# Attention + max3-MoE on one Trainium2 core: the rounding of a finished pv moved one step later, and left keys times v moved to column halves of TensorE

## Chip, cores and metric

One Trainium2 chip, 1 core. The metric is device microseconds of one execution. The kernel before takes 641.23 us (median of 3 runs, 640.48 to 642.72).

## The reference

Attention with a relative-position bias over 4 batches, 8 heads, 576 positions, head size 64, in fp32, and then an MoE-like layer on the 2304 tokens:

```
scores = q @ k.T / 8 + bias            # bias: a small MLP of log-distances, one 576x576 map per head
attn   = exp(scores - max); attn /= sum + 1e-9
x      = attn @ v                      # tokens x 512
h      = max(x @ w1, x @ w2, x @ w3)   # 2304 x 768
out    = h @ w_out                     # 2304 x 512
```

## The kernel before

The program runs in three stages: bias maps (to about 57 us), attention (to about 340 us), and the MoE layer. The change touches attention alone.

Attention works on 16 **units**, one for each pair of heads and batch. A unit has five **steps**, t0 to t4, one for each tile of 128 queries. Steps t0 to t3 handle 128 queries of both heads; t4 handles the last 64 queries of both heads as one tile. So a step has two score tiles (h0 and h1), and t4 has one. The program is written out in a fixed order for each engine (`step`, L325), and engines work through their own lists in that order. A step n does, across engines:

- TensorE: `front` (L234), the score matmuls **s** of step n, in three terms because q and k are split into a rounded part and a remainder; then `flip` (L286, L295), the transposes **tp** and **lp** of the step three back; then, if some are queued, two or three **pairs** of pv matmuls (L311, L314).
- VectorE: `shift` (L244), which reads s out of PSUM, adds the bias and finds the extreme (**sn**, **nm**), once per head; the sum's reciprocal **rc** of the step before (L263, L264); a copy of transposed tiles to **et** (L359). Every third step of the later attention also has two operations that convert MoE weights (L385 to L401).
- ScalarE: the exponentials **e** (L256) and copies to et (L341, L357). GpSimd: the product e times rc (L267) and the splitting of the next unit's q and k (L201, L203).

**pv**, the product with v, is done in two groups per unit: queries 0 to 255 (group 0, 256 wide) and 256 to 575 (group 1, 320 wide). A group is queued after the flip of its last tile and consists of five pairs: four chunks of 128 keys and one of the 64 left keys. A pair is two matmuls, one per head, which write to the lower and the upper 64 partitions of the one PSUM buffer `pv` (there is one, of one bank; all eight banks are in use). Group 1 of a unit runs in steps t3 (three pairs) and t4 (two) of the next unit, group 0 in t0 (three) and t1 (two) of the next. So one group ends in t4 and the next begins in t0; the other ends in t1 and the next begins in t3.

The four chunks use 128 rows of TensorE and 64 columns per head (tiles of 128 x 64, L311). The left keys lie on partitions 0 to 63 for one head and 64 to 127 for the other, so their pair uses 64 rows and 64 columns per head (L314). After a group's fifth pair, at the end of the same step, ScalarE rounds pv to **xhi** (L317) and VectorE writes the remainder **xlo** (L318). v of the next unit is loaded in t4 (`load_v`, L206).

Of the kernel before, what the change touches and what calls it, by code (L numbers as in the profile page):

```python
# [9 lines left out]
F32 = mybir.dt.float32  # L10
# [3 lines left out]
ALU = mybir.AluOpType  # L14
# [5 lines left out]
def kernel(  # L20
# [12 lines left out]
    nc = tc.nc  # L33
    B, H, S, D = v.shape
# [3 lines left out]
    NTQ = S // 128  # L38
    LB = 128 * NTQ
    LEFT = S - LB  # L40
# [6 lines left out]
    psum = ctx.enter_context(tc.tile_pool(name="psum", bufs=1, space=PSUM))  # L47
    dram = ctx.enter_context(tc.tile_pool(name="dram", bufs=1, space=DRAM))

    def ps_s(name):  # L50
        return psum.tile([128, 2, 512], F32, tag="s", bufs=2, name=name)
# [6 lines left out]
    xhi = []  # L58
    xlo = []
# [97 lines left out]
    def load_bias(hp, t):  # L157
        if t < NTQ:
            nc.sync.dma_start(out=bias_t[t], in_=bias_rows(128 * t, 128, 2 * hp, 0, S, 2))
        else:  # L160
            nc.sync.dma_start(out=bias_t[t][0:LEFT], in_=bias_rows(LB, LEFT, 2 * hp, 0, S))
            nc.sync.dma_start(out=bias_t[t][64:64 + LEFT, 0:LB], in_=bias_rows(LB, LEFT, 2 * hp + 1, LEFT, LB))
            nc.sync.dma_start(out=bias_t[t][64:64 + LEFT, LB:S], in_=bias_rows(LB, LEFT, 2 * hp + 1, 0, LEFT))
# [3 lines left out]
    units = [(hp, b) for hp in range(HP) for b in range(B)]  # L167
# [7 lines left out]
    class Attention:  # L175
        def __init__(self, pool):
            self.pool = pool
            self.data = {}
            self.st = {}
            self.et = {}  # L180
            self.pvq = []
            bias_t.extend(pool.tile([128, 2, S], F32, name=f"bias{t}", bufs=1) for t in range(NTQ))
            bias_t.append(pool.tile([128, S], F32, name="biasm", bufs=1))

# [21 lines left out]
        def load_v(self, un):  # L206
            pool, (hp, b) = self.pool, units[un]
            vt = pool.tile([128, NTQ, 2, D], F32, tag="vt", bufs=2, name=f"vt{un}")
            vl = pool.tile([128, D], F32, tag="vl", bufs=2, name=f"vl{un}")
            for h in range(2):  # L210
                main, left = (0, LB) if h == 0 else (LEFT, 0)
                src = v[b, 2 * hp + h]
                nc.sync.dma_start(out=vt[:, :, h], in_=src[main:main + LB].rearrange("(c p) d -> p c d", p=128))
                nc.sync.dma_start(out=vl[64 * h:64 * h + LEFT], in_=src[left:left + LEFT])
            self.data[un].update(vt=vt, vl=vl)

        def heads(self, n):
# [80 lines left out]
                nc.tensor.transpose(lp[0:64], e2[:, LB:S], ident)  # L298
            return tps, (el[:, c0:c0 + m], lp[:, 0:m])

        def queue_pv(self, un, c0, w, ea, el):
            hp, b = units[un]
            u = self.data[un]
            pv = psum.tile([128, w], F32, tag="pv", bufs=1, name=f"pv{un}_{c0}")

            def pair(c):
                def run():
                    for h in range(2):
                        p = slice(64 * h, 64 * h + 64)
                        if c < NTQ:  # L310
                            nc.tensor.matmul(pv[p], lhsT=u["vt"][:, c, h], rhs=ea[:, c, h],  # L311
                                             start=(c == 0), stop=False)
                        else:
                            nc.tensor.matmul(pv[p], lhsT=u["vl"][p], rhs=el[p], start=False, stop=True)  # L314
                    if c == NTQ:
                        r = slice(b * S + c0, b * S + c0 + w)
                        nc.scalar.copy(xhi[hp][:, r], pv)  # L317
                        nc.vector.tensor_tensor(out=xlo[hp][:, r], in0=pv, in1=xhi[hp][:, r].bitcast(F32),  # L318
                                                op=ALU.subtract)
                return run  # L320

            self.wait = True
            self.pvq.extend(pair(c) for c in range(NTQ + 1))

        def step(self, n, more=None):  # L325
            m, f = n - 1, n - LAG
            nh = 0
            if n < NSTEP:
                un, t = sched[n]
                hp, b = units[un]  # L330
                if t == 0 and un + 2 < len(units):
                    self.load_qk(un + 2)
                if t == 4 and un + 1 < len(units):
                    self.load_v(un + 1)
                nh = self.heads(n)
                self.front(n)
                self.shift(n, 0)
            back = 0 <= f < NSTEP
            if back:
                tps, left = self.flip(f)  # L340
                nc.scalar.copy(*tps[0])  # L341
            if nh:
                self.expo(n, 0)
            if nh > 1:
                self.shift(n, 1)
            if n < NSTEP and b == B - 1 and hp + 1 < HP:
                load_bias(hp + 1, t)
            if 0 <= m < NSTEP:
                self.norm(m)
            if nh > 1:  # L350
                self.expo(n, 1)
            if n < NSTEP and un + 1 < len(units):
                if t == 0:
                    self.splits = self.prep(un + 1)
                next(self.splits, None)
            if back:
                nc.scalar.copy(*left)  # L357
                if len(tps) > 1:
                    nc.vector.tensor_copy(*tps[1])  # L359
            if more is not None:  # L360
                for _ in range(2):
                    next(more, None)
            k = 3 if len(self.pvq) >= 3 else 2
            run, self.pvq = self.pvq[:k], self.pvq[k:]
            for x in run:
                x()
            if back:
                un, t = sched[f]
                g = 0 if t < TS else 1
                w = 128 * TS if g == 0 else S - 128 * TS  # L370
                del self.st[f]
                if t in (TS - 1, NS - 1):
                    self.queue_pv(un, 128 * TS * g, w, *self.et)
# [32 lines left out]
    def load_w(pool, wpool, f):  # L406
        for i, m in enumerate((mw1, mw2, mw3)):
            hi = pool.tile([128, KDM * 128], F32R, tag=f"wh{i}", bufs=1, name=f"wh{i}_{f}")
            lo = pool.tile([128, KDM * 128], F32R, tag=f"wl{i}", bufs=1, name=f"wl{i}_{f}")
            wf[i, f] = (hi, lo)  # L410
            src = m[:, 256 * f:256 * f + 256].rearrange("(c p) f -> p c f", p=128)
            yield from convert(wpool, src, hi, lo, f"{i}_{f}")
# [72 lines left out]
    with tc.manual_schedule():  # L485
        nc.vector.memset(signm, 0x80000000)
        warm = const.tile([128, 256], F32, name="warm")
        nc.vector.memset(warm, 0.0)
        wps = ps_s("wps")
        for _ in range(5):  # L490
            nc.tensor.matmul(wps[:, 0, 0:256], lhsT=warm[:, 0:128], rhs=warm, start=True, stop=True)
        apool = tc.alloc_tile_pool(name="attn_p", bufs=1, side="right")
        at = Attention(apool)
        n = 0
        with tc.tile_pool(name="bias_p", bufs=1) as bp:
            for g, _ in enumerate(bias_stage(bp)):
                if g == 0:
                    at.load_qk(0)
                    at.load_v(0)
                    first = at.prep(0)  # L500
                if 5 <= g < 9:
                    next(first)
                if g == 16:
                    at.load_qk(1)
                if g in (10, 18, 26, 34):
                    load_bias(0, g // 8 - 1)
                if g >= NG:
                    at.step(n)
                    n += 1
            load_bias(0, NTQ)  # L510
        xpool = ctx.enter_context(tc.tile_pool(name="xpool", bufs=1, reuse_waits="tile"))
        wpool = ctx.enter_context(tc.tile_pool(name="wpool", bufs=1, reuse_waits="tile"))
        xhi.extend(xpool.tile([128, NT], F32R, name=f"xhi{i}") for i in range(HP))
        xlo.extend(xpool.tile([128, NT], F32R, name=f"xlo{i}") for i in range(HP))
        w0 = load_w(wpool, wpool, 0)
        while n < NSTEP + LAG:
            at.step(n, w0 if n >= NSTEP - 57 and n % 3 == 0 else None)
            n += 1
        while at.pvq:
            at.pvq.pop(0)()  # L520
        for _ in w0:
            pass
        apool.release()
        with tc.tile_pool(name="moe_p", bufs=1, reuse_waits="tile") as mp:
            for _ in moe(mp, wpool):
                pass
# [54 lines left out]
```

## Time and profile before

| | |
|---|---|
| runs | 641.23 us median, 640.48 to 642.72 |
| profiled execution, its own time | 641.89 us |
| its span in the profile | 640.0 us |
| TensorE busy | 612.2 us, 96% of the span |
| VectorE, ScalarE, GpSimd busy | 61%, 43%, 29% |
| mean granted TensorE clock | 0.984 of full speed |

Busy shares are means over three different stages. What an edit of attention is worth is read from the timeline of a step: which wait ends last there. In the views, PE is TensorE's matmuls, PEld its weight loads, DVE is VectorE, ACT ScalarE, POOL GpSimd, SPq the queue that issues DMAs.

### The profile page before, as it was taken

What the parts mean: (1) busy time and instruction counts of PE and PEld (TensorE: products, weight loads), DVE (VectorE), ACT (ScalarE), POOL (GpSimd) and SP (SyncE); (2) the same over time, 40 slices, a digit from 0 to 9 for tenths busy, and PEclk for the clock granted to TensorE, in tenths of its full rate; (3) what the DMA queues carried; (4) which work ended last, traced back from release to release, by engine and by line L of the source; (5) the groups of instructions that cost most, each with busy time, mean ns of one, the idle gap of its engine ahead of it and who ended that gap; (6) DMA issues with size and microseconds to landing.
All of it is one profiled execution on the core that took longest, in us unless ns stands there. A gap on an engine that the chain in (4) does not pass through costs nothing.

```text
span 640.0 us, 11424 instructions
## 1 busy us (share of the span) xinstructions
PE 612.2 (96%) x4248; PEld 460.4 (72%) x4248; DVE 388.1 (61%) x996; ACT 272.4 (43%) x708; POOL 186.3 (29%) x216
## 2 busy tenths in 40 slices
PE   6987999999999989999999999999999999999997
PEld 3333766666666666666667898989889898988886
DVE  7995766666867787688754464746556464133331
ACT  4986666666657666666661000000000001034443
POOL 3020666666766666666640000000000000000000
PEclk7998899999989999999999999999999999999999
DMA  4887522522163224620101131211213110001111
GB/s 111 255 291 242 182 60 59 174 75 89 55 199 112 61 61 134 185 61 19 52 2 34 34 96 36 66 34 67 66 34 98 34 67 1 1 33 67 67 66 68
DMA packets 47864, 55.17 MB, mean 86 GB/s; under 512 B 21952, under 2 KB 31424, under 8 KB 47808
## 3 DMA queue, kind: packets, MB, share of 16 engines
q1 hardware_dynamic: 47808, 54.43, 27.4%
q8 instruction: 34, 0.56, 0.4%
q14 instruction: 22, 0.18, 0.1%
HBM read 38.81 MB, written 15.61 MB: 85 GB/s over the span
## 4 chain that ended last, share of the span: by engine, by line
PE 81%; DVE 7%; ACT 6%; DMA 3%; issue 2%; POOL 0%; DVEq 0%; ACTq 0%; SPq 0%
PE s L234 10%; PE pv L311 10%; PE tp L286 9%; PE h L454 8%; PE h L456 8%; PE h L455 8%; DVE sn L244 4%; PE g L454 4%; PE g L456 4%; PE g L455 4%; PE o L480 4%; PE o L478 4%; PE o L479 4%; PE bp L127 3%; ACT e L256 3%; DMA bias_d<-bs 2%
## 5 line engine op out<-in xcount | busy, mean ns | idle before, releaser
L267 POOL TENSOR_SCALAR e<-e,rc 128x576 f32<-128x576 f32 x144 | 109.1, 769 | 116.7 <-DVE rc L264 73.3
L256 ACT ACTIVATE e<-sn,nm 128x576 f32<-128x576 f32 x144 | 110.6, 771 | 8.6 <-DVE nm L244 8.5
L244 DVE CUSTOM_DVE_ANT_0 sn<-s,bias 128x576 f32<-128x576 f32 x128 | 91.7, 754 | 31.0 <-PE s L234 30.6
L461 ACT COPY m<-h 128x512 f32<-128x512 f32 (+1 forms) x30 | 16.4, 546 | 202.8 <-PE h L456 183.8
L456 PE MATMUL h<-xhi,wl 128*128 128x512 f32 (+1 forms) x240 | 88.3, 368 | 0.0
L454 PE MATMUL h<-xhi,wh 128*128 128x512 f32 (+1 forms) x240 | 88.3, 368 | 0.0
L455 PE MATMUL h<-xlo,wh 128*128 128x512 f32 (+1 forms) x240 | 88.2, 368 | 0.0
L341 ACT COPY et<-tp 128x512 f32<-128x512 f32 x80 | 46.9, 587 | 84.0 <-PE tp L286 84.0
L286 PE MATMUL tp<-ident,e 128*128 128x128 f32 x576 | 81.0, 282 | 0.0
L234 PE MATMUL s<-kh,qh 64*128 64x288 f32 (+1 forms) x288 | 66.9, 351 | 13.9 <-DVE nm L244 13.2
L311 PE MATMUL pv<-et,vt 128*64 128x320 f32 (+1 forms) x512 | 76.9, 422 | 0.5 <-ACT et L341 0.5
L234 PEld LDWEIGHTS s<-kh,qh 64*128 64x128 f32 (+1 forms) x288 | 37.0, 189 | 49.2 <-DVE nm L244 22.4
L286 PEld LDWEIGHTS tp<-ident,e 128*128 128x128 f32 x576 | 63.8, 142 | 11.4 <-issue 8.3
L234 PE MATMUL s<-kl,qh 64*128 64x288 f32 (+1 forms) x288 | 55.5, 307 | 0.7 <-POOL kl L203 0.7
L234 PE MATMUL s<-kh,ql 64*128 64x288 f32 (+1 forms) x288 | 52.8, 296 | 0.0
L127 PE MATMUL bp<-hid,w2s 128*32 128x79 f32 (+48 forms) x640 | 43.6, 412 | 7.9 <-DVE hid L106 3.9
L433 DVE TENSOR_TENSOR hl<-ht,hh 128x128 fp32r<-128x128 f32 x108 | 23.4, 286 | 44.8 <-ACT hh L432 44.8
L462 DVE TENSOR_TENSOR m<-h,m 128x512 f32<-128x512 f32 (+1 forms) x30 | 19.2, 638 | 50.7 <-ACT m L461 50.3
L454 PEld LDWEIGHTS h<-xhi,wh 128*128 128x128 f32 x240 | 45.1, 188 | 6.2 <-issue 0.5
L311 PEld LDWEIGHTS pv<-et,vt 128*64 128x64 f32 x512 | 31.5, 137 | 24.8 <-issue 11.0
L455 PEld LDWEIGHTS h<-xlo,wh 128*128 128x128 f32 x240 | 45.0, 188 | 5.7
L456 PEld LDWEIGHTS h<-xhi,wl 128*128 128x128 f32 x240 | 45.0, 188 | 5.7
(74 smaller groups left out, 1063.7 us busy)
## 6 DMA issues: line engine op xcount, KB each, us to landing
bias_d<-bs SPq DMA_DIRECT2D x36, 295.5 KB, 4.9
bias<-bias_d SPq DMA_DIRECT2D x16, 576.0 KB, 4.2
w<-in_moe_w_dram SPq DMA_DIRECT2D x18, 512.0 KB, 3.6
qr<-in_qd_dram SPq DMA_DIRECT2D x16, 320.0 KB, 3.4
kr<-in_kd_dram SPq DMA_DIRECT2D x16, 320.0 KB, 3.5
out_dram<-ot SPq DMA_DIRECT2D x17, 256.0 KB, 2.0
vt<-in_v_dram SPq DMA_DIRECT2D x32, 128.0 KB, 2.4
w64o<-in_moe_w_out_dram SPq DMA_DIRECT2D x6, 512.0 KB, 3.3
```

The source lines that it names most:

```text
L127: nc.tensor.matmul(bp[32 * c:32 * c + 32, o:o + w], lhsT=w2s, rhs=src, start=True, stop=True)
L234: nc.tensor.matmul(ss[h][:, x, 0:HALF], lhsT=u[q][p, r], rhs=u[k][p, c:c + HALF], start=(j == 0), stop=(j == 2))
L244: nc.vector.tensor_tensor_reduce(out=sn.rearrange("p (a b) -> p a b", a=2), in0=st["s"][h][:, :, 0:HALF], in1=bt.rearrange("p (a b) -> p a ...
L256: nc.scalar.activation(st["e"][:, S * h:S * h + S], sn, ACTF.Exp, scale=-1.0, bias=nm, accum_out=st["sm"][:, h:h + 1])
L267: nc.gpsimd.tensor_scalar(out=e, in0=e, scalar1=rc[:, h:h + 1], scalar2=1.0, op0=ALU.mult, op1=ALU.mult)
L286: nc.tensor.transpose(tp[:, 128 * c:128 * c + 128], e2[:, k0:k0 + 128], ident)
L311: nc.tensor.matmul(pv[p], lhsT=u["vt"][:, c, h], rhs=ea[:, c, h], start=(c == 0), stop=False)
L341: nc.scalar.copy(*tps[0])
L454: nc.tensor.matmul(o, lhsT=hi[:, r], rhs=x, start=(c == 0), stop=False)
L455: nc.tensor.matmul(o, lhsT=hi[:, r], rhs=y, start=False, stop=False)
L456: nc.tensor.matmul(o, lhsT=lo[:, r], rhs=x, start=False, stop=(c == KDM - 1))
L478: nc.tensor.matmul(po, lhsT=hh[:, f], rhs=woh[:, f, r], start=(f == 0), stop=False)
```

## The change

After a group's fifth pair nothing is issued any more; the finished pv is noted in `done`. `high()` (xhi, ScalarE) runs at the start of the next step, ahead of ScalarE's first copy there; `low()` (xlo, VectorE) runs in the next step behind both `shift` calls. The first pair of a group calls both (they then have nothing left to do, except behind the last step) and only then takes the buffer `pv`. v's left keys of the two heads now lie in one tile of 128 partitions x 2 x 64, zero on the half of the other head, so that their matmuls use 128 rows and 64 columns like the chunks. The zeros are written once, by two GpSimd memsets; two such tiles alternate between units. The load of v moves from t4 of the unit before to t1 of the unit itself.

```diff
+            self.done = []
+            self.vl = [pool.tile([128, 2, D], F32, name=f"vl{x}", bufs=1) for x in range(2)]
+            for x in self.vl:
+                nc.gpsimd.memset(x, 0.0)
...
-            vl = pool.tile([128, D], F32, tag="vl", bufs=2, name=f"vl{un}")
+            vl = self.vl[un % 2]
...
-                nc.sync.dma_start(out=vl[64 * h:64 * h + LEFT], in_=src[left:left + LEFT])
+                nc.sync.dma_start(out=vl[64 * h:64 * h + LEFT, h], in_=src[left:left + LEFT])
...
-            pv = psum.tile([128, w], F32, tag="pv", bufs=1, name=f"pv{un}_{c0}")
+            made = []
             def pair(c):
                 def run():
+                    if c == 0:
+                        self.high()
+                        self.low()
+                        made.append(psum.tile([128, w0], F32, tag="pv", bufs=1, name=f"pv{un}_{c0}"))
+                    pv = made[0]
                     for h in range(2):
                         p = slice(64 * h, 64 * h + 64)
-                        if c < NTQ:
-                            nc.tensor.matmul(pv[p], lhsT=u["vt"][:, c, h], rhs=ea[:, c, h],
-                                             start=(c == 0), stop=False)
-                        else:
-                            nc.tensor.matmul(pv[p], lhsT=u["vl"][p], rhs=el[p], start=False, stop=True)
+                        w, x = (u["vt"][:, c, h], ea[:, c, h]) if c < NTQ else (u["vl"][:, h], el)
+                        nc.tensor.matmul(pv[p], lhsT=w, rhs=x, start=(c == 0), stop=(c == NTQ))
                     if c == NTQ:
-                        r = slice(b * S + c0, b * S + c0 + w)
-                        nc.scalar.copy(xhi[hp][:, r], pv)
-                        nc.vector.tensor_tensor(out=xlo[hp][:, r], in0=pv, in1=xhi[hp][:, r].bitcast(F32),
-                                                op=ALU.subtract)
+                        self.done.append([pv, hp, slice(b * S + c0, b * S + c0 + w0)])
...
+        def high(self):
+            for x in self.done:
+                if len(x) == 3:
+                    pv, hp, r = x
+                    nc.scalar.copy(xhi[hp][:, r], pv)
+                    x.append(True)
+
+        def low(self):
+            for pv, hp, r, _ in self.done:
+                nc.vector.tensor_tensor(out=xlo[hp][:, r], in0=pv, in1=xhi[hp][:, r].bitcast(F32),
+                                        op=ALU.subtract)
+            self.done = []
 
         def step(self, n, more=None):
             m, f = n - 1, n - LAG
             nh = 0
+            self.high()
...
-                if t == 4 and un + 1 < len(units):
-                    self.load_v(un + 1)
+                if t == 1 and un:
+                    self.load_v(un)
...
             if nh > 1:
                 self.shift(n, 1)
+            self.low()
...
         while at.pvq:
             at.pvq.pop(0)()
+        at.high()
+        at.low()
```

VectorE around the change from t4 to t0 (names end in buffer numbers; `sn_0` and `sn_1` are the two heads' sn, `pv_256` is group 1, `pv_0` group 0). Before:

```order
210 L264 RECIPROCAL rc_1563<-sm_1511 128x2
211 L359 COPY et_0_1496<-tp_1_1_1552 128x4x128
212 L318 TENSOR_TENSOR xlo_927<-pv_256_1478,xhi_923 128x320
213 L244 ISA sn_0_1595,nm_0_1596<-s_0_0_1581,bias_81 128x576
214 L244 ISA nm_0_1596 128x1
215 L244 ISA sn_1_1615,nm_1_1616<-s_0_1_1582,bias_81 128x576
216 L244 ISA nm_1_1616 128x1
217 L263 TENSOR_SCALAR sm_1561<-sm_1561 128x1
218 L264 RECIPROCAL rc_1619<-sm_1561 128x1
```

And the same place in the changed kernel:

```order
210 L268 RECIPROCAL rc_1558<-sm_1511 128x2
211 L377 COPY et_0_1496<-tp_1_1_1547 128x4x128
212 L248 ISA sn_0_1588,nm_0_1589<-s_0_0_1574,bias_85 128x576
213 L248 ISA nm_0_1589 128x1
214 L248 ISA sn_1_1608,nm_1_1609<-s_0_1_1575,bias_85 128x576
215 L248 ISA nm_1_1609 128x1
216 L337 TENSOR_TENSOR xlo_930<-pv_256_1525,xhi_926 128x320
217 L267 TENSOR_SCALAR sm_1556<-sm_1556 128x1
218 L268 RECIPROCAL rc_1613<-sm_1556 128x1
```

The remainder xlo of group 1 moved from ahead of both sn to behind both. In t2 the remainder of group 0 moves in the same way.

TensorE in the same step t0, from the last transpose to the first pair of group 0 and the scores of t1, with what each waits for (a semaphore per engine or DMA queue). Before:

```order
577 L295 MATMUL lp_2_1609<-ident,e_1462 128x128 [waits Activation_49]
578 L311 MATMUL pv_0_1576<-et_0_1496,vt_1282 64x256 [waits DMAHW4_49,DVE_49]
579 L311 MATMUL pv_0_1576<-et_0_1496,vt_1282 64x256 [waits DMAHW6_49]
580 L311 MATMUL pv_0_1576<-et_0_1496,vt_1282 64x256 x4
581 L234 MATMUL s_1_0_1635<-kh_1474,qh_1374 128x288 [waits DVE_49]
```

And in the changed kernel:

```order
579 L299 MATMUL lp_2_1602<-ident,e_1462 128x128 [waits Activation_49]
580 L320 MATMUL pv_0_1623<-et_0_1496,vt_1381 64x256 [waits DMAHW6_49,DVE_49,PE_49]
581 L320 MATMUL pv_0_1623<-et_0_1496,vt_1381 64x256 [waits DMAHW0_49]
582 L320 MATMUL pv_0_1623<-et_0_1496,vt_1381 64x256 x4
583 L238 MATMUL s_1_0_1635<-kh_1475,qh_1369 128x288 [waits PE_49]
```

TensorE's own order is the same. Its first pair of group 0 waits for VectorE in both kernels, and the operation that it waits for, the xlo that reads the buffer, now stands behind both sn of the same step.

## Rows read from the trace of the kernel before

**Rows 1.** The page: busy time of TensorE (us, share of the span, instructions), and its granted clock in 40 slices of 16 us, in tenths of full speed.

```profile
PE 612.2 (96%) x4248; PEld 460.4 (72%) x4248; DVE 388.1 (61%) x996; ACT 272.4 (43%) x708; POOL 186.3 (29%) x216
PEclk7998899999989999999999999999999999999999
```

**Rows 2.** The page: shares of the span of the chain of work that ended last, by engine.

```profile
PE 81%; DVE 7%; ACT 6%; DMA 3%; issue 2%; POOL 0%; DVEq 0%; ACTq 0%; SPq 0%
```

**Rows 3.** Timeline, from the last two pv pairs of group 1 in a step t4 through t0 to the first s of t1. Columns: start (us), time (us), engine, line, operation, out<-in, count, and the engine's idle time before it with what ended it.

```profile
209.45 0.76 PE L311 MATMUL pv<-et,vt 128*64 128x320 f32 x4
...
210.14 0.76 PE L314 MATMUL pv<-et,vl 64*64 64x320 f32 x4
...
210.83 0.40 PE L234 MATMUL s<-kh,qh 64*128 64x288 f32 x2
...
210.94 0.43 ACT L317 CAST xhi<-pv 128x320 fp32r<-128x320 f32 x1 [0.42 <-PE pv L314]
...
211.40 0.49 DVE L318 TENSOR_TENSOR xlo<-pv,xhi 128x320 fp32r<-128x320 f32 x1 [0.82 <-ACT xhi L317]
...
211.93 0.76 DVE L244 CUSTOM_DVE_ANT_0 sn<-s,bias 128x576 f32<-128x576 f32 x1
...
212.61 0.75 DVE L244 CUSTOM_DVE_ANT_0 sn<-s,bias 128x576 f32<-128x576 f32 x1
...
212.96 1.52 PE L311 MATMUL pv<-et,vt 128*64 128x256 f32 x12
...
213.29 0.15 DVE L263 TENSOR_SCALAR sm<-sm 128x1 f32<-128x1 f32 x1
...
213.90 0.75 POOL L267 TENSOR_SCALAR e<-e,rc 128x576 f32<-128x576 f32 x1 [2.23 <-DVE rc L264]
...
214.40 0.40 PE L234 MATMUL s<-kh,qh 64*128 64x288 f32 x2
```

**Rows 4.** Timeline, same columns, from the last two pairs of group 0 in a step t1 through t2 and t3 to the first s of t4.

```profile
199.64 0.65 PE L311 MATMUL pv<-et,vt 128*64 128x256 f32 x4
...
200.22 0.65 PE L314 MATMUL pv<-et,vl 64*64 64x256 f32 x4
...
200.80 0.40 PE L234 MATMUL s<-kh,qh 64*128 64x288 f32 x2
...
201.77 0.42 DVE L318 TENSOR_TENSOR xlo<-pv,xhi 128x256 fp32r<-128x256 f32 x1 [0.78 <-ACT xhi L317]
...
202.11 0.75 DVE L244 CUSTOM_DVE_ANT_0 sn<-s,bias 128x576 f32<-128x576 f32 x1
...
202.92 0.40 PE L234 MATMUL s<-kh,qh 64*128 64x288 f32 x1 [0.26 <-DVE nm L244]
...
205.72 1.83 PE L311 MATMUL pv<-et,vt 128*64 128x320 f32 x12
...
207.48 0.40 PE L234 MATMUL s<-kh,qh 128*128 128x288 f32 x1
```

**Rows 5.** Waits: engine and line, what it waited for, us in total, times, longest us.

```profile
PEld pv L314 <- issue: 14.0, 32, 0.5
PE s L234 <- DVE nm L244: 13.2, 34, 1.4
```

**Rows 6.** All weight loads of the four chunks (L311): duration in ns, lowest, median, highest.

```profile
L311 PEld LDWEIGHTS pv<-et,vt x512: 132/137/232, 75.4 to 339.0; 128*64 128x64 f32 x171
```

**Rows 7.** Timeline of a step t2 whose VectorE list has weight conversions ahead of xlo, to the first s of t3 and of t4.

```profile
183.27 0.41 DVE L318 TENSOR_TENSOR xlo<-pv,xhi 128x256 fp32r<-128x256 f32 x1
183.60 0.74 DVE L244 CUSTOM_DVE_ANT_0 sn<-s,bias 128x576 f32<-128x576 f32 x1
...
184.41 0.39 PE L234 MATMUL s<-kh,qh 64*128 64x288 f32 x1 [1.16 <-DVE nm L244]
...
185.08 0.40 PE L234 MATMUL s<-kh,qh 64*128 64x288 f32 x1 [0.29 <-DVE nm L244]
...
190.60 0.40 PE L234 MATMUL s<-kh,qh 128*128 128x288 f32 x1
```

**Rows 8.** Timeline of TensorE: the first s of t3 in the other two such places.

```profile
237.86 0.40 PE L234 MATMUL s<-kh,qh 64*128 64x288 f32 x1 [1.43 <-DVE nm L244]
...
289.42 0.40 PE L234 MATMUL s<-kh,qh 64*128 64x288 f32 x1 [1.17 <-DVE nm L244]
```

**Rows 9.** Timeline of the two steps t0 with weight conversions ahead of xlo.

```profile
247.23 0.48 DVE L318 TENSOR_TENSOR xlo<-pv,xhi 128x320 fp32r<-128x320 f32 x1
...
247.63 0.74 DVE L244 CUSTOM_DVE_ANT_0 sn<-s,bias 128x576 f32<-128x576 f32 x1
...
247.89 1.52 PE L311 MATMUL pv<-et,vt 128*64 128x256 f32 x12
...
298.81 0.47 DVE L318 TENSOR_TENSOR xlo<-pv,xhi 128x320 fp32r<-128x320 f32 x1
```

**Rows 10.** Timeline of POOL at the program's start.

```profile
0.73 0.20 POOL masks.py:197 MEMSET ident<- 128x128 f32 x1 [0.29 <-POOLq L538]
...
5.03 0.93 POOL L201 CAST qh<-qr 128x640 fp32r<-128x640 f32 x1 [3.25 <-DMA qr<-in_qd_dram]
```

**Rows 11.** Waits of the DMA queue: line, what it waited for, us in total, times, longest us.

```profile
SPq L213 <- PE pv L311: 155.3, 14, 15.4
```

**Rows 12.** Engines in a stretch: time, busy us (instructions) of each, granted TensorE clock, DMA share, GB/s.

```profile
186.40:189.80 3.40, 3.40 (x16) 2.18 (x16) 2.09 (x7) 2.26 (x6) 2.92 (x5) 0.50 0.79 228
```

More of the change, by code (lines that the diff above doesn't have):

```diff
@@ L299, in flip, with queue_pv @@
             return tps, (el[:, c0:c0 + m], lp[:, 0:m])
-        def queue_pv(self, un, c0, w, ea, el):
+        def queue_pv(self, un, c0, w0, ea, el):
             hp, b = units[un]
             u = self.data[un]
-            pv = psum.tile([128, w], F32, tag="pv", bufs=1, name=f"pv{un}_{c0}")
+            made = []
             def pair(c):
                 def run():
+                    if c == 0:
[3 more added lines that the diff above has]
+                    pv = made[0]
                     for h in range(2):
                         p = slice(64 * h, 64 * h + 64)
-                        if c < NTQ:
-                            nc.tensor.matmul(pv[p], lhsT=u["vt"][:, c, h], rhs=ea[:, c, h],
-                                             start=(c == 0), stop=False)
-                        else:
-                            nc.tensor.matmul(pv[p], lhsT=u["vl"][p], rhs=el[p], start=False, stop=True)
+                        w, x = (u["vt"][:, c, h], ea[:, c, h]) if c < NTQ else (u["vl"][:, h], el)
+                        nc.tensor.matmul(pv[p], lhsT=w, rhs=x, start=(c == 0), stop=(c == NTQ))
                     if c == NTQ:
-                        r = slice(b * S + c0, b * S + c0 + w)
-                        nc.scalar.copy(xhi[hp][:, r], pv)
-                        nc.vector.tensor_tensor(out=xlo[hp][:, r], in0=pv, in1=xhi[hp][:, r].bitcast(F32),
-                                                op=ALU.subtract)
+                        self.done.append([pv, hp, slice(b * S + c0, b * S + c0 + w0)])
                 return run
```

## The prediction, made before the changed kernel was run

> **What bounds the kernel now.** I read the engine table, the chain, the timeline of one unit, and the waits, in this order. TensorE is busy for 96% of the span [rows 1], and the chain that ended last is 81% TensorE and 7% VectorE [rows 2]. So work taken off TensorE counts in full where TensorE has no gap, and a gap counts in full too, since nothing later makes it up. Which of the two holds has to be read step by step.
>
> From t4 to t1 TensorE has no gap [rows 3]: the last chunk's pair at 209.45, the left keys' pair at 210.14, the scores of t0 at 210.83, transposes, the first three pairs of the next group at 212.96, the scores of t1 at 214.40. VectorE's xlo runs from 211.40 to 211.89, while it would otherwise wait for these scores: sn of h0 starts at 211.93, which is 1.10 us after the first s. So in t0 the present place of xlo costs nothing, and its buffer is free 1.07 us before pv's first pair needs it.
>
> From t1 to t3 it is different [rows 4]. s of t2 starts at 200.80, and sn of h0 at 202.11, 1.31 us later instead of 1.10: xlo (201.77) is in its way by 0.21 us. TensorE has little to do in t2 and runs dry: s of t3 for h0 starts at 202.92, 0.06 us after that sn ended (202.86) and after 0.26 us of idle time. In all, scores stood idle for VectorE's nm for 13.2 us [rows 5]. Here VectorE sets the pace.
>
> **Left keys on column halves.** The count of matmuls stays: 4 instructions for a pair, 32 pairs of left keys. What goes is one change of tile form. Three pairs of width 256 and the way to the next s take 214.40 - 212.96 = 1.44 us [rows 3]; one pair and the change to the left keys' form takes 200.22 - 199.64 = 0.58, and the left keys' pair and the change to s again 200.80 - 200.22 = 0.58 [rows 4]. With d for a pair and c for a change, 3d + c = 1.44 and d + c = 0.58 give d = 0.43 and c = 0.15. Width 320 gives the same: 3d + c = 1.76 [rows 4], d + c = 0.69 [rows 3], so d = 0.535, c = 0.155. The new pair is a fifth pair like the four, so one c of 0.15 goes per group. Its bounds: nothing, or the whole idle time of the weight loads ahead of it, 14.0 / 32 = 0.44 us [rows 5]. I take 0.15, since most of that 0.44 is matmul time of the pair before, which stays. It counts wherever s of the next step leads the path: 32 places, less the 5 below where weight conversions on VectorE lead; 27 x 0.15 = **-4.1 us** (bounds 0 and -11.9).
>
> A row speaks for the pair's price: 12 weight loads of 0.137 us [rows 6] would be 1.64 us one after another, and the three pairs that they belong to take 1.44 with the change [rows 3], so loads on 128 rows run beside the matmuls. The Trainium skill, page "TensorE: Matmul & The Clock Gate", Part 3, section "The mechanism", says that a weight load overlaps running matmuls only where its row group differs, and the new left pair gives up different row groups; by that rule the loads would come into the open. The trace does not agree with it for the chunks' pairs.
>
> **xlo behind sn in t2.** 15 units have this step with scores (group 0 of the last unit ends behind them). sn starts 0.21 us earlier, and s of t3 with it: in 12 of them 0.21. In 3, weight conversions keep VectorE until after the scores [rows 7, 8]; there the whole slot of xlo, 183.60 - 183.27 = 0.33 us, goes ahead of sn. 12 x 0.21 + 3 x 0.33 = **-3.5 us**. What moves later is the reciprocal, by 0.13 us net (xlo's slot of 202.11 - 201.77 = 0.34, less the 0.21), and POOL's product with it; it is transposed two steps on.
>
> **xlo behind sn in t0.** This is the expensive one. There is one pv buffer, and group 0's first pair has to wait until xlo of group 1 has read it. xlo now starts where VectorE is free behind sn of h1, which is where sm starts today: 213.29 [rows 3]. It takes 0.49, to 213.78, and TensorE follows 0.06 us after VectorE as at 202.92 [rows 4]: 213.84, against 212.96 now. TensorE stands 0.88 us with everything else of its list behind it: three pairs, then s of t1. Nothing gives it back, because t1 has no gap and t3's gap hangs on sn of t2, which moves with s of t2. 14 units have this step. In 12: 0.88 each. In 2, conversions delay sn: it starts where xlo stands today, 247.23, and xlo comes 2 x 0.68 later (the spacing of the two sn in [rows 3]), 248.59, ends 0.49 later, and pv starts at 249.14 instead of 247.89 [rows 9]: 1.25 each. 12 x 0.88 + 2 x 1.25 = **+13.1 us**. Bounds per place: 0.73, if the release comes at the end of xlo's slot (247.63 - 247.23 = 0.40 instead of 0.49) and without the 0.06; 1.03 if it is as much slower; so +11.0 to +15.2.
>
> **The rest, at nothing.** xhi keeps its place in ScalarE's list: the end of one step and the start of the next are neighbours there. In t0 the reciprocal and POOL's product (213.90 [rows 3]) move by 0.41 us; that product is transposed two steps later, and the et copy is needed by a group that starts three steps later. If that cover were gone, it would cost another 14 x 0.41 = 5.7. Two memsets like the one of 0.20 us run before POOL waits 3.25 us for its first load [rows 10]; without that cover 0.4 us once. The load of v issued in t4 held the DMA queue for its buffer, 155.3 us in all [rows 11]; in t1 that buffer is free, the loads behind it go out earlier, and v has four steps until use.
>
> **Sum.** -4.1 - 3.5 + 13.1 = +5.5 us on the profiled execution's 641.89, so 647.4. That execution stands 0.66 above the median of 641.23; I predict a median of **646.7 us**, slower by 0.9%.
>
> **Rivals.**
> - **The wait is covered (faster).** If TensorE came to pv's first pair 0.88 us later anyway, because its transposes in t0 waited for e or for a free tp buffer, the +13.1 would vanish: 646.7 - 13.1 = 633.6. It decides from the point at which TensorE would reach that pair at 213.84 or later on the clock of [rows 3]. Against it: TensorE is without a gap from 210.83 to 212.96 today. Chance 0.05.
> - **The change of form costs the full 0.44.** Then 27 x 0.44 = 11.9 instead of 4.1, and 638.9. For it: the idle row [rows 5]. Against it: 3d + c. Chance 0.06, half of it faster, half within 0.3%.
> - **The clock falls in the new gaps.** After idle times of 1.16 and 0.29 us [rows 7] the granted clock fell to 0.50 (1.2 GHz) for a while [rows 12], and the step took 190.60 - 184.41 = 6.19 us instead of 207.48 - 202.92 = 4.56 [rows 4]: 1.63 us lost. After 1.43 and 1.17 [rows 8] it stayed at 2.4 GHz [rows 1]. A gap of 0.88 is smaller than any of these, the two of 1.25 are not. If every third new gap did it, 5 x 1.63 = 8.2, and 654.9. Chance 0.11. In the forecast I let the one fall of today, whose gap shrinks by 0.33, stand against one at the gaps of 1.25.
> - **Weight loads of the left pair in the open.** 4 loads x 32 x 0.137 [rows 6] = 17.5 us, and 664.2. It is the skill's rule above as a mechanism of this kernel; the chunks' pairs speak against it. Chance 0.03.
>
> **How the numbers follow.** Forecast 0.75, with 644 to 650 as its own range, of which 0.06 lies within 0.3% (1.9 us, about what a measurement of this kernel can tell from no change; 639.3 to 643.1). Faster: 0.05 + 0.03 = 0.08. Within: 0.06 + 0.03 = 0.09. Slower: 0.69 + 0.11 + 0.03 = 0.83. The range of 642.5 to 652.5 takes in the bounds of the stall (2.1 either way), a larger saving of the change of form, and up to three falls of the clock; it leaves out the first two rivals and the far ends of the others.
>
> **What would show it.** Right: in t0 of the changed kernel the first pair of group 0 has some 0.8 us idle before it, released by VectorE's xlo, in 14 places, two of them longer; left keys' pair and fifth chunk follow without idle weight loads, and last chunk to next s takes 2d + c = 1.01 us at width 256 instead of 1.16; in t2 sn starts 1.10 us after s, and the gap before s of t3 shrinks to about 0.05. Wrong: no idle time before pv in t0, or a granted clock that falls in many units, or transposes that now wait for POOL.

## Result, and the profile after

The changed kernel takes 648.04 us (median of 6 runs, 646.52 to 652.67) against 641.35 us for the kernel before (6 runs): ratio 1.0115, 95% interval [1.0079, 1.0151]. In a second set, run together with some of the experiments, it was 647.85 us, ratio 1.0099 [1.0086, 1.0113]. It is slower by about 1%; 646.7 was forecast. Its profiled execution took 647.13 us, 5.24 more than that of before. Two executions stand far from all others and are left out of the ratios: one of the run mid (3246.56 us at a granted clock of 0.167) and one of the kernel before beside the second set (752.78 us at 0.749).

The page of the changed kernel: TensorE is busy for 3.4 us less than before [rows 1] in a span that is 5.4 us longer, and the chain that ended last has 5% in which an engine waited for nothing that the profile names, against 2% [rows 2].

```profile
PE 608.8 (94%) x4248; PEld 465.9 (72%) x4248; DVE 393.2 (61%) x996; ACT 272.2 (42%) x708; POOL 184.8 (29%) x218
...
PE 85%; DVE 6%; issue 5%; ACT 2%; DMA 1%; POOL 0%; DVEq 0%; ACTq 0%
```

The timeline of the changed kernel from t4 through t0 to t1, to be laid beside [rows 3] (start, time, engine, line, operation, out<-in, count, idle time before and its releaser):

```profile
209.65 0.76 PE L320 MATMUL pv<-et,vt 128*64 128x320 f32 x4
...
210.24 0.71 PE L320 MATMUL pv<-et,vl 128*64 128x320 f32 x4
...
210.88 0.40 PE L238 MATMUL s<-kh,qh 64*128 64x288 f32 x2
...
211.02 0.42 ACT L332 CAST xhi<-pv 128x320 fp32r<-128x320 f32 x1 [0.30 <-PE pv L320]
...
211.97 0.76 DVE L248 CUSTOM_DVE_ANT_0 sn<-s,bias 128x576 f32<-128x576 f32 x1 [0.87 <-PE s L238]
...
212.65 0.75 DVE L248 CUSTOM_DVE_ANT_0 sn<-s,bias 128x576 f32<-128x576 f32 x1
...
212.79 0.27 PE L299 MATMUL lp<-ident,e 128*128 128x128 f32 x1
...
213.33 0.49 DVE L337 TENSOR_TENSOR xlo<-pv,xhi 128x320 fp32r<-128x320 f32 x1
...
213.92 1.52 PE L320 MATMUL pv<-et,vt 128*64 128x256 f32 x12 [0.85 <-PE lp L299]
...
215.36 0.40 PE L238 MATMUL s<-kh,qh 64*128 64x288 f32 x2
```

The reader is to see the new gap: lp ends at 213.06, pv starts at 213.92, 0.10 us after xlo ends (213.82). The step is 215.36 - 210.88 = 4.48 us long instead of 3.57. The row names lp as the releaser, but lp had ended 0.85 us before; pv waits for several semaphores, and of the engines that it waits for, only VectorE had something to finish there. The waits list repeats the wrong name, with the size of the damage:

```profile
PE pv L320 <- PE lp L299: 10.2, 12, 0.9
PE s L238 <- DVE nm L248: 10.1, 23, 1.2
```

The second row is the gain: 10.1 us in 23 waits instead of 13.2 in 34 [rows 5]. It comes from t2. The timeline of the changed kernel from t1 through t2 to t3, beside [rows 4]:

```profile
200.18 0.65 PE L320 MATMUL pv<-et,vt 128*64 128x256 f32 x4
...
200.67 0.60 PE L320 MATMUL pv<-et,vl 128*64 128x256 f32 x4
...
201.20 0.40 PE L238 MATMUL s<-kh,qh 64*128 64x288 f32 x2
...
202.30 0.76 DVE L248 CUSTOM_DVE_ANT_0 sn<-s,bias 128x576 f32<-128x576 f32 x1 [0.76 <-PE s L238]
...
203.12 0.40 PE L238 MATMUL s<-kh,qh 64*128 64x288 f32 x1
...
203.66 0.42 DVE L337 TENSOR_TENSOR xlo<-pv,xhi 128x256 fp32r<-128x256 f32 x1
...
203.80 0.40 PE L238 MATMUL s<-kh,qh 64*128 64x288 f32 x1 [0.28 <-DVE nm L248]
```

sn of h0 now starts 1.10 us after s, not 1.31; s of t3 follows without idle time before h0. The last chunk and the left keys' pair to the next s take 201.20 - 200.18 = 1.02 us, not 1.16.

Both traces cut into steps (from the first s of one step to that of the next) and compared step by step give the account of the span:

| part | difference, us |
|---|---|
| t0: 12 x 0.915, 1.11, 1.73 | +13.8 |
| t1 and t4: 29 steps, -0.145 each | -4.2 |
| t2: 12 x -0.205, 3 x -0.19 | -3.0 |
| last steps, without scores | -0.45 |
| t3: one fall of the clock in either (-1.64 and +1.54), the rest +0.05 | 0 |
| first unit of attention, of which t1 -0.63 | -0.7 |
| bias stage -0.15, MoE +0.13 | 0 |
| sum (span 640.0 to 645.4) | +5.4 |

### The profile page after: what moved, and what is told of

Read it like the earlier page. It is cut to its first block, busy times and chain, and to the rows that moved or that the text cites. A ratio compares the mean times of both kernels' runs of the same rounds, so it can differ in the third digit from the quotient of the medians.

```text
span 645.4 us, 11453 instructions
## 1 busy us (share of the span) xinstructions
PE 608.8 (94%) x4248; PEld 465.9 (72%) x4248; DVE 393.2 (61%) x996; ACT 272.2 (42%) x708; POOL 184.8 (29%) x218
## 4 chain that ended last, share of the span: by engine, by line
PE 85%; DVE 6%; issue 5%; ACT 2%; DMA 1%; POOL 0%; DVEq 0%; ACTq 0%
PE pv L320 13%; PE s L238 12%; PE tp L290 9%; PE h L472 8%; PE h L474 8%; PE h L473 8%; PE g L473 4%; PE g L474 4%; PE g L472 4%; PE o L498 4%; PE o L497 4%; PE o L496 4%; PE bp L127 3%; DVE sn L248 3%; DVE hid L106 2%
## 5 line engine op out<-in xcount | busy, mean ns | idle before, releaser
L238 PE MATMUL s<-kh,qh 64*128 64x288 f32 (+1 forms) x288 | 66.7, 349 | 11.3 <-DVE nm L248 10.1
L290 PEld LDWEIGHTS tp<-ident,e 128*128 128x128 f32 x576 | 64.1, 143 | 11.4 <-issue 10.1
L320 PEld LDWEIGHTS pv<-et,vt 128*64 128x64 f32 x512 | 33.3, 136 | 36.2 <-PE lp L299 12.7
L127 PE MATMUL bp<-hid,w2s 128*32 128x79 f32 (+48 forms) x640 | 45.1, 426 | 6.7 <-DVE hid L106 3.5
```

The costliest lines, as they stand in the source:

```text
L127: nc.tensor.matmul(bp[32 * c:32 * c + 32, o:o + w], lhsT=w2s, rhs=src, start=True, stop=True)
L238: nc.tensor.matmul(ss[h][:, x, 0:HALF], lhsT=u[q][p, r], rhs=u[k][p, c:c + HALF], start=(j == 0), stop=(j == 2))
L290: nc.tensor.transpose(tp[:, 128 * c:128 * c + 128], e2[:, k0:k0 + 128], ident)
L320: nc.tensor.matmul(pv[p], lhsT=w, rhs=x, start=(c == 0), stop=(c == NTQ))
```

## Experiments

My theory: the loss is TensorE's wait for xlo of the group before, as long as xlo is late on VectorE; the left keys and t2 gain. Rivals: the gaps cost through the granted clock; the left keys' form or the moved load of v costs.

**left_only.** xlo back ahead of both sn, the rest as changed.

```diff
             self.high()
+            self.low()
...
                 self.shift(n, 1)
-            self.low()
```

> The changed kernel, but with VectorE's xlo back at its old place in the list, ahead of both sn; left keys on column halves and the load of v in t1 stay. My account: 32 changes of tile form less at 0.145 us each, so 4.6 us faster than before (about 636.8), no idle time before pv in t0, and sn of t2 still 1.31 us after s. Rival, weight loads of the left pair come into the open or the moved load costs: no gain or a loss. Rival, a change of form costs the full 0.44 us: 14 us faster.

Measured 637.53 us, ratio 0.9944 [0.9922, 0.9966]: faster, so neither the new form nor the moved load costs. The trace corrects the sum, though. t4 steps are 0.145 us shorter, and t1 steps too, but t2 steps are 0.15 longer than before. The timeline of left_only in t1 and t2 shows why:

```profile
196.04 0.60 PE L320 MATMUL pv<-et,vl 128*64 128x256 f32 x4
...
196.57 0.40 PE L238 MATMUL s<-kh,qh 64*128 64x288 f32 x2
...
197.28 0.38 ACT L332 CAST xhi<-pv 128x256 fp32r<-128x256 f32 x1
...
197.69 0.42 DVE L337 TENSOR_TENSOR xlo<-pv,xhi 128x256 fp32r<-128x256 f32 x1 [0.78 <-ACT xhi L332]
...
198.03 0.75 DVE L248 CUSTOM_DVE_ANT_0 sn<-s,bias 128x576 f32<-128x576 f32 x1
```

xhi has no idle time before it: ScalarE comes to it when its own list lets it, not when pv is done. So xlo and sn stay where they are when s comes 0.15 us sooner, and sn starts 1.46 us after s. The gain of t1 counts only with xlo out of sn's way. By the steps left_only gains 2.5 us. The ratio says 3.6; the rest would fit the clock: the profiled execution of before had one fall (1.63 us) more, and of the timed executions 5 of 6 of left_only stand at a granted clock of 0.987, but 10 of 11 of before at 0.984.

**move_only.** xhi and xlo one step later, left keys and load of v as before.

```diff
-                        w, x = (u["vt"][:, c, h], ea[:, c, h]) if c < NTQ else (u["vl"][:, h], el)
+                        w, x = (u["vt"][:, c, h], ea[:, c, h]) if c < NTQ else (u["vl"][p], el[p])
...
-                if t == 1 and un:
-                    self.load_v(un)
+                if t == 4 and un + 1 < len(units):
+                    self.load_v(un + 1)
```

> The changed kernel with the left keys' pair and the load of v as before; only xhi and xlo are issued one step later, xlo behind both sn. My account: 14 gaps before pv in t0, +13.8 us, and sn of t2 earlier, -3.1 us: 10.7 us slower than before (about 652). Rival, the loss lies in the left keys' new form or the moved load: no slower than before.

Measured 651.44 us, ratio 1.0153 [1.0134, 1.0171]: the loss is there in full without the left keys' edit. Its twelve t0 without conversions are 0.92 us longer than before, the two with conversions 1.59 each; no fall of the clock stands in its trace behind the first unit. Its TensorE timeline from t4 to t1 has the old pair, 211.70 to 212.38 = 0.68 us (0.64 in the changed kernel), and the same gap:

```profile
211.70 0.76 PE L317 MATMUL pv<-et,vl 64*64 64x320 f32 x4
212.38 0.40 PE L235 MATMUL s<-kh,qh 64*128 64x288 f32 x2
...
215.43 1.52 PE L317 MATMUL pv<-et,vt 128*64 128x256 f32 x12 [0.85 <-PE lp L296]
216.88 0.40 PE L235 MATMUL s<-kh,qh 64*128 64x288 f32 x2
```

**split.** As changed, but in t0 xlo stands ahead of both sn.

```diff
             self.high()
+            if n < NSTEP and sched[n][1] == 0:
+                self.low()
```

> The changed kernel with one difference: in t0 xlo stands ahead of both sn as before; in t2 it stays behind them. My account: the gap of t0 goes with its +13.8 us and the two gains stay, 4.6 + 3.1, so 7.7 us faster than before (about 633.6). Rival, the gaps matter through the granted clock and not through their own length: the same time, but then fill (the gap filled with work) should also be as fast as this.

Measured 634.39 us, ratio 0.9883 [0.9868, 0.9899]: faster than both kernels, as expected within 0.8 us. One t0 with conversions stays 0.33 us longer than before (last section). In its timeline of t0 xlo lies in VectorE's free time while TensorE computes the scores, and the step is 211.15 - 207.57 = 3.58 us long:

```profile
207.57 0.40 PE L238 MATMUL s<-kh,qh 64*128 64x288 f32 x2
...
208.17 0.49 DVE L337 TENSOR_TENSOR xlo<-pv,xhi 128x320 fp32r<-128x320 f32 x1 [0.37 <-ACT xhi L332]
...
208.67 0.76 DVE L248 CUSTOM_DVE_ANT_0 sn<-s,bias 128x576 f32<-128x576 f32 x1
...
209.70 1.51 PE L320 MATMUL pv<-et,vt 128*64 128x256 f32 x12
...
211.15 0.40 PE L238 MATMUL s<-kh,qh 64*128 64x288 f32 x2
```

**mid and mid_again.** xlo between the two sn.

```diff
+            self.low()
             if nh > 1:
                 self.shift(n, 1)
-            self.low()
```

> The changed kernel with xlo between the two sn, in t0 and t2. My account, priced by VectorE's position: in t0 xlo starts 0.68 us sooner than behind both, so the gap falls from 0.91 to about 0.23 us, 14 x 0.23 = +3.2; in t2 s of t3 for h0 comes sooner, but its h1 waits for the second sn, which ends as before, so nothing is gained there; with the left keys' 4.6 us: 1.4 us faster than before (about 640). Rival, the wait is for something other than xlo: the gap stays at 0.91, about 649.

Measured 644.11 us, ratio 1.0038 [1.0026, 1.0050]. I was 4 us off, so it ran once more, for its trace:

> xlo between the two sn, for its profile; the time was 644.1 where I had expected 640. My account now: in t2 xlo cannot start before the first sn is through, and the second sn, which h1 of t3 waits for, ends later than before: 1.10 + 0.68 + 0.34 = 2.12 us after s instead of 1.98; with s of t2 itself earlier by 0.15 through the left keys, which that wait then gives back in part. So t2 is 2.25 us long instead of 1.91, 15 times, and the gap in t0 is 0.23. Rival: the gap in t0 is larger than 0.23.

Measured 643.38 us, ratio 1.0038 [1.0019, 1.0057]. In mid_again, the timeline of TensorE in t0:

```profile
211.19 1.52 PE L320 MATMUL pv<-et,vt 128*64 128x256 f32 x12 [0.17 <-PE lp L299]
```

The timeline of VectorE there, with the first sn and xlo:

```profile
209.92 0.76 DVE L248 CUSTOM_DVE_ANT_0 sn<-s,bias 128x576 f32<-128x576 f32 x1 [1.20 <-PE s L238]
...
210.60 0.48 DVE L337 TENSOR_TENSOR xlo<-pv,xhi 128x320 fp32r<-128x320 f32 x1
```

And the timeline of TensorE around t2 and t3, the last two s:

```profile
200.73 0.40 PE L238 MATMUL s<-kh,qh 64*128 64x288 f32 x1
...
201.74 0.40 PE L238 MATMUL s<-kh,qh 64*128 64x288 f32 x1 [0.61 <-DVE nm L248]
```

The rule of the theory holds: xlo starts 0.68 us after the first sn, pv follows 0.11 us behind its end, and t0 is 0.24 us longer than before instead of 0.915 (12 steps; the two with conversions 0.44 and 0.74). What I had missed is t2: TensorE waits once for each head, and the wait for the second sn lasts 0.61 us instead of 0.28. t2 is 0.20 shorter and t3 0.33 longer, 15 x 0.13 = 2.0 us worse than before. The second account had the size, but put it into t2; it stands in t3.

**load_only.** The kernel before, v loaded in t1 of its own unit.

```diff
-                if t == 4 and un + 1 < len(units):
-                    self.load_v(un + 1)
+                if t == 1 and un:
+                    self.load_v(un)
```

> The kernel before with one edit: v of a unit is loaded in its own t1 instead of t4 of the unit before. My account: no difference (641.4). Rival, the DMA queue's waits of 155.3 us for v's buffer held up loads that somebody waits for: 1 us or more faster; or v comes late for pv: slower by the wait, with idle time before the first pv pair of t0.

Measured 642.02 us, ratio 1.0012 [0.9997, 1.0026]: no difference. The waits of the DMA queue for v's buffer, 155.3 us before [rows 11], fall to 29.8 us in 2 waits, and the steps from the second unit's t1 on keep their lengths, so those 155.3 us cost nothing.

**after_again and fill.** The changed kernel, and the same with TensorE kept busy in the gap.

```diff
+                for _ in range(9 if t == 2 and un else 1):
                     nc.tensor.transpose(lp, e2[:, LB:S + LEFT], ident)
```

> The changed kernel once more, beside the three others of this set. 646.5 to 652, with a mean granted clock between 0.976 and 0.989 that goes with the time: longer where the clock is lower.

> The changed kernel with the gap ahead of pv in t0 filled: the left keys' transpose of that step is done nine times instead of once, into the same place, 8 x 0.107 us = 0.86 for a gap of 0.85; nothing else changes. If the gaps cost their own length alone, the median stays within 0.5 us of the changed kernel's in this set, and so does the spread. If gaps also lower the granted clock in some executions, the slowest runs go: spread of 2 us as before the change, median 1 to 2 us lower.

Measured: after_again 647.85 us (646.58 to 648.57), fill 650.38 (648.16 to 651.21), ratio to before 1.0133 [1.0115, 1.0151]. Fill is not faster; it is 2.5 us slower than after_again, where at most 0.5 was expected. Its TensorE timeline in t0:

```profile
213.83 0.40 PE L238 MATMUL s<-kh,qh 64*128 64x288 f32 x2
...
215.75 1.15 PE L300 MATMUL lp<-ident,e 128*128 128x128 f32 x9
216.87 1.52 PE L321 MATMUL pv<-et,vt 128*64 128x256 f32 x12
218.32 0.40 PE L238 MATMUL s<-kh,qh 64*128 64x288 f32 x2
```

The gap is filled, and the step is 218.32 - 213.83 = 4.49 us long as with the gap. From the second unit's t0 (the sixth step) to the start of the last step with scores, the traces take 261.93 us in fill and 261.86 in after_again, each with one fall of the clock, after the same step. So in these two executions the gap costs its own length and nothing through the clock. Fill's extra time lies elsewhere: 0.87 us in the last steps, where the eight extra transposes have no gap to hide in, and in its profiled execution 2.1 ahead of the first step with pv, where the two kernels do the same work. Of these, 1.2 are t0 and t1 of the first unit, where the granted clock stood at 0.50 for 10.24 us against 6.83 in after_again. Whether the timed executions differ for the same reason is open.

## Why the prediction was right

**The wait in t0** was priced by VectorE's place in time: 12 x 0.88 and 2 x 1.25, +13.1. Measured 12 x 0.915, 1.11 and 1.73, +13.8. The hand-over from VectorE took 0.10 us instead of 0.06. split shows that the wait is the loss (it goes, and the kernel is faster than both), mid_again that it scales with xlo's place, fill that its length is its price. The first rival, a cover for the wait, failed as its point of decision said: TensorE reached pv 0.85 us too early. The two places with conversions were not understood, though. The prediction left the conversions where they stood; in fact they start 0.31 us later in one place and 0.31 us sooner in the other (last section). The one that is sooner stands behind a fall of the clock; move_only, without a fall, has 1.59 in both. So 1.25 is some 0.3 us too small for an execution without a fall, and that the two places add up to 2.84 for a forecast of 2.5 is in part luck.

**The left keys and t2** were priced at -4.1 and -3.5, together -7.6; measured -4.2 (t1, t4), -0.45 (last steps) and -3.0 (t2), together -7.7. Change of form 0.145 us for a forecast 0.15; sn earlier by 0.21 as forecast; the rival with 0.44 us fell, and so did that with weight loads in the open. The prediction left out the five places in which conversions lead, and rightly: the 0.145 us is gained there too, but the next step gives it back. The three t2 with conversions are 0.19 us shorter instead of 0.33, and the two t0 are longer by 0.145 for it. In the twelve other units the two gains add up only because xlo has moved. That is what my expectation of left_only missed: there t2 gives t1's gain back.

**The clock.** Behind the first unit of attention the granted clock fell once to 0.50 (1.2 GHz) in the profiled execution of either kernel: before in the t3 behind 1.16 us of idle time [rows 7], after in the t3 at 238.92, behind 1.24 us. The number is as forecast, the place is not: the forecast had the new fall at the t0 gaps of 1.25 us. None of the twelve gaps of 0.85 us was followed by a fall, nor those of 1.05 and 1.66 us in t0. In the nine profiled executions there are eight such falls, all in a t3 behind a t2 with conversions. The timed executions of the first set reach 650.70 and 652.67 us, both at a granted clock of 0.976, the other four at 0.984 to 0.989; those of the second stay below 648.6. Nothing shows that the gaps cause the long ones; one execution of fill, whose gaps are filled, stands at 0.976 too (651.21 us). The question stays open.

**The sum** came closer than its terms, by luck. The rows of the table that the edit makes (t0, t1 and t4, t2, last steps) add up to +6.1 us where +5.5 was forecast; the first unit of attention takes 0.7 back. There the granted clock stood at 0.50 for 10.24 us before and for 6.82 us after. The edit does not set this: split, mid_again and fill, which do the same work in that unit as the changed kernel, have 10.24 us, and load_only, which has neither the new left keys nor the moved xlo, has 6.83. The median was forecast 0.66 us below the profiled execution, as before; it lies 0.91 above, hence 648.04 for 646.7. The stretches, with the fall in t3 behind them (columns as in [rows 12]), first of before, then of the changed kernel:

```profile
60.10:70.34 10.24, 8.67 (x44) 6.74 (x45) 5.84 (x20) 5.32 (x14) 5.12 (x6) 0.50 0.76 248
```

```profile
62.59:69.41 6.82, 5.84 (x32) 4.82 (x32) 4.21 (x16) 3.38 (x9) 5.11 (x6) 0.50 0.90 320
240.08:243.49 3.41, 3.41 (x20) 2.67 (x18) 2.57 (x8) 1.93 (x7) 2.59 (x4) 0.50 0.32 96
```

The first s of the t3 in which it fell, in the timeline of the changed kernel:

```profile
238.92 0.39 PE L238 MATMUL s<-kh,qh 64*128 64x288 f32 x1 [1.24 <-DVE nm L248]
```

**At nothing** was right for the load of v, though its buffer was not always free in t1: the queue still stood for it 32.7 us in 6 waits in the changed kernel. It was right for xhi, which starts 0.14 us after s in t0 and 0.11 before. What the memsets cost cannot be told: attention starts at 57.05 us instead of 57.20, and anywhere from 56.1 to 58.7 in the nine traces. For the later reciprocal in t2 it was wrong by 0.3 us where conversions lead a t0 that has no fall of the clock before it (last section).

## What to carry to other kernels

Moving an operation behind more urgent ones on its engine is only free if the buffer that it reads is not wanted sooner: look for who writes that buffer next, and compare its start with the end of the moved operation. The same move can gain in one step of a loop and lose in another; here one condition that keeps t0 as it was turned a loss of 1% into a gain of 1.2%. Two small gains that hang on the same wait are to be priced together.

## What the runs showed of the hardware

A VectorE operation held by GpSimd. The row of sm (L263, L267), a tensor_scalar on two elements per partition, takes 0.15 us in t0, but in t3 and t4 it lasts until just behind the end of a GpSimd operation that splits k. In the trace of before, 31 of its 81 rows take over 0.3 us, and all of these but the first end 0.02 to 0.03 us behind the end of a GpSimd operation; of the rows that meet no GpSimd operation, none but that first takes over 0.17 us.

In the changed kernel kl of GpSimd comes 0.99 us after s of t4 in most units, not 0.67, and sm there lasts 0.3 us longer. The cause is that xlo of t2 now stands ahead of the reciprocal, and with it of GpSimd's product: with xlo back at its old place (left_only) kl is at 0.67 again, and in split and move_only, with xlo late in t2, at 0.99. The timelines of before and, under them, of the changed kernel, in t4:

```profile
208.15 1.56 POOL L203 TENSOR_TENSOR kl<-kr,kh 128x640 fp32r<-128x640 f32 x1
...
209.26 0.47 DVE L263 TENSOR_SCALAR sm<-sm 128x2 f32<-128x2 f32 x1
```

```profile
208.66 1.55 POOL L207 TENSOR_TENSOR kl<-kr,kh 128x640 fp32r<-128x640 f32 x1
...
209.46 0.78 DVE L267 TENSOR_SCALAR sm<-sm 128x2 f32<-128x2 f32 x1
```

The ends are 209.71 and 209.73 before, 210.21 and 210.24 after. The Trainium skill, page "SBUF — State Buffer", section "Who interferes with whom", says that VectorE and GpSimd share a pair of ports, and that when VectorE works in a two-port mode, whichever issues first has the pair for its whole instruction and the other is blocked. The rows agree; in which mode sm worked, none of them shows.

The traces also have places without GpSimd's operation. Where a fall of the clock makes t3 some 1.6 us longer, kl has ended before sm of t4 begins. In all eight places of this kind sm takes 0.16 to 0.17 us. In the changed kernel one of them is the t4 ahead of the t0 of 1.11 us; the t4 ahead of the t0 of 1.73 us has no fall before it. Both have conversions. Their timelines, the first:

```profile
244.46 1.55 POOL L207 TENSOR_TENSOR kl<-kr,kh 128x640 fp32r<-128x640 f32 x1
...
246.79 0.17 DVE L267 TENSOR_SCALAR sm<-sm 128x2 f32<-128x2 f32 x1
...
247.73 0.72 DVE L417 CAST wh<-wa 128x512 fp32r<-128x512 f32 x1
```

And the second:

```profile
299.04 1.54 POOL L207 TENSOR_TENSOR kl<-kr,kh 128x640 fp32r<-128x640 f32 x1
...
299.83 0.78 DVE L267 TENSOR_SCALAR sm<-sm 128x2 f32<-128x2 f32 x1
...
301.38 0.98 DVE L414 SCALAR_TENSOR_TENSOR wa<-w,signm,wt 128x512 uint32<-128x512 uint32 x1
```

s of t4 starts at 245.02 and 298.05, so the conversions start 2.71 and 3.33 us after it; before, 3.02 in both places. sn, xlo and pv stand behind them. With the 1.25 us of the forecast and the 0.145 us by which s of t0 comes sooner, this makes 1.09 and 1.71 us, for the measured 1.11 and 1.73.
